# Seven-product gated FFN on one core: T1 in four sums, fifth products side by side, ScalarE copies and buffers moved, a later T4 sum, one copy for the last tile

## The chip, the cores and the metric

The kernel runs on one core of one Trainium2 chip. Its time is device time in microseconds (us), the median of the runs shown. Engines are named as the profile names them: PE (matmul, with its weight loads as PEld), DVE (VectorE), ACT (ScalarE), POOL (GpSimd), SP (the DMA queue of SyncE; ACT has a queue too).

## The reference, cut to what matters

```
x: 1024 tokens x 1024 (D)   w_gate, w_up: 1024 x 3584 (F)   w_down: 3584 x 1024      all bf16
out = (gelu_tanh(x @ w_gate) * (x @ w_up)) @ w_down
```

## The kernel before, in words

Both matrix stages use the seven-product form of a 2x2 block product (Strassen's, in Winograd's variant) in place of eight products; the block sums that it needs are made by DVE, POOL and ACT.

**Stage 1** makes gate and up together. For each of the 28 blocks of 128 columns of F (index i), the block matrix A has the gate weights for the two halves of D (a11, a12) and the up weights for the same halves (a21, a22). B is x transposed: B11 and B21 are the two halves of D for tokens 0 to 511 (tile xt0), B12 and B22 the same for tokens 512 to 1023 (tile xt1). xt0 and xt1 come by two DMA transposes on SP. Each product is four matmuls (KH = 4 slices of 128 rows of D) into one PSUM bank of 128x512. Sums of B are made once: T1 = B12 - B11, T2 = B22 - T1, T3 = B22 - B12, T4 = B21 - T2 (`t_sum`, line 153, on DVE), and an fp32 copy of B22 (line 264, on ACT). Sums of A are made for each block: S1, S3 (`early_sums`, lines 165 and 166), S2 (line 170), S4 (line 174), and C22, a copy of a22 (`copy_a22`, line 177, on ACT). Per block:

- `first_product` (a11 x B11) goes to PSUM bank A, and ACT copies it to E1 (line 186). `second_product` (a12 x B21) is added in the same bank, so it can start only when that copy has read it; then ACT's gelu gives the gate of the first tokens (line 192).
- `seed` (line 198): ACT writes E1 into another bank, X. On X are added in turn the sixth product (S2 x T2; ACT copies the bank to E2, line 213), the seventh (S3 x T3; copied to e3, line 226) and the fourth (C22 x T4; DVE multiplies it with the gate, line 217).
- The fifth product (S1 x T1) opens bank Y. DVE adds e3 to it, which is u1 (line 228); the third product (S4 x B22) is added in Y; DVE adds E2 to it, which is h1 (line 233); ACT takes its gelu (line 235) and DVE multiplies it with u1 (`finish`, line 238).

The order of every engine is written out by hand: each engine runs its instructions in program order, and semaphores join them. Eight blocks (LEAD) have their first and second products before anything else, in pairs: first n, first n+1, second n, second n+1. `ahead` then gives one first and one second product at a time. After LEAD, blocks 0 and 1 go together (fifth, ahead, sixth, seventh, ahead, fourth, third), and from block 2 on a loop does one block at a time. PSUM has eight banks: four (tag p) for warm-up and X, four (tag q) for A and Y in turn. e3 has one buffer, u1 three, h1 two.

**Stage 2** is out = hidden x w_down, with 14 pairs of F blocks as two halves of 7 (JF), four token tiles of 128 (TT) and two column halves of w_down. A product is 56 matmuls (line 359). DVE makes, in this order around the change: new sums for the second chain (lines 414, 415), S4 (line 432), T4 in seven pieces (`t4_sum`, line 389), then T3 and S3 in rings of four buffers (`t3_sum` line 386, `s3_sum` line 382), then the output sums (`store_sum`, line 373). The last product but one (S3 x T3, on X) holds back its last two steps of j (TAIL = 2) to the end; the last product (56 matmuls, t by t) is then added on X, copied to bf16 and sent. Its last tile is copied in halves, one by ACT and one by DVE, and sent in two DMAs of 64 KB.

Of the kernel before, what the change touches and what calls it, by code (L numbers as in the profile page):

```python
# [7 lines left out]
ACT = mybir.ActivationFunctionType  # L8
# [4 lines left out]
def kernel(  # L13
# [18 lines left out]
    nc = tc.nc  # L32
    P = nc.NUM_PARTITIONS
    fp32 = mybir.dt.float32
    f32r = mybir.dt.float32r
    bf16 = mybir.dt.bfloat16

    xf = x.flatten_outer_dims()
    of = out.flatten_outer_dims()
    N, D = xf.shape  # L40
    F = w_gate.shape[1]
    NB = 512
    DT = D // P
    KH = DT // 2
    FT = F // P
    NT = N // P
    DB = 512
    NDB = D // DB
    assert N == 2 * NB and DT % 2 == 0 and D % DB == 0 and FT % 4 == 0
    NWARM = 18  # L50
# [3 lines left out]
    TT = NT // 2  # L54
    JF = KF // 2
# [16 lines left out]
    epool = stage1.enter_context(tc.tile_pool(name="e", bufs=2))  # L72
# [3 lines left out]
    B11, B21 = xt0[:, :KH, :], xt0[:, KH:, :]  # L76
    xt1 = uw.tile([P, DT, NB], bf16, name="xt1", tag="uw")
    B12, B22 = xt1[:, :KH, :], xt1[:, KH:, :]
    WG, WU = {}, {}

    def load_gate(c, queue, lo=0, hi=DT):
        if c not in WG:
            WG[c] = gw.tile([P, DT, 2 * P], bf16, name="gw", tag="gw")
        queue.dma_start(  # L84
            out=WG[c][:, lo:hi, :], in_=wg_r[:, lo:hi, 2 * c * P : (2 * c + 2) * P]
        )
# [15 lines left out]
    def a12(i):  # L102
        return block(WG, 2, i, 1)
# [4 lines left out]
    def a22(i):  # L108
        return block(WU, 4, i, 1)

    def product(ps, lhs, rhs, first=True):
        for k in range(KH):
            nc.tensor.matmul(  # L113
                ps,
                lhsT=lhs[:, k, :],
                rhs=rhs[:, k, :],
                start=(first and k == 0),
                stop=(k == KH - 1),
                skip_group_check=True,
            )  # L120

    def psum_p(name):
        return psum.tile([P, NB], fp32, name=name, tag="p")

    def psum_q(name):
        return psum.tile([P, NB], fp32, name=name, tag="q")

    with tc.manual_schedule():
        zt = opool.tile([P, NB], bf16, name="zt", tag="o")
        nc.vector.memset(zt, 0.0)  # L130
        warm = [psum_p("warm") for _ in range(4)]
        for n in range(NWARM):
            nc.tensor.matmul(warm[n % 4], lhsT=zt[:, 0:P], rhs=zt, start=True, stop=True)

        table = opool.tile([P, 8], bf16, name="table", tag="o")
        nc.scalar.activation(table, zt[:, 0:8], ACT.Gelu_apprx_tanh)

        nc.sync.dma_start_transpose(out=xt0, in_=xf[0:NB, :])  # L138
        load_gate(0, nc.scalar, 0, KH)
        load_gate(0, nc.sync, KH, DT)  # L140
        load_gate(1, nc.sync)
        load_up(0, 0, 2)
# [6 lines left out]
        T = {}  # L149
        for name in ("T1", "T2", "T3", "T4", "B22"):  # L150
            T[name] = xpool.tile([P, KH, NB], f32r, name=name, tag=name)

        def t_sum(name, a, b):
            for k in range(0, KH, 2):
                ks = slice(k, k + 2)
                nc.vector.tensor_tensor(T[name][:, ks, :], a[:, ks, :], b[:, ks, :], ALU.subtract)  # L156

        S1, S2, S3, S4, C22 = {}, {}, {}, {}, {}
# [13 lines left out]
        def late_sums(i, engine=nc.gpsimd):  # L172
            S4[i], C22[i] = weight_tile("s4"), weight_tile("c22")
            engine.tensor_tensor(S4[i], a12(i), S2[i], ALU.subtract)  # L174

        def copy_a22(i):
            nc.scalar.activation(C22[i], a22(i), ACT.Copy)
# [3 lines left out]
        def first_product(i):  # L181
            A[i] = psum_q("a")
            product(A[i], a11(i), B11)
            if i % 2 == 0:
                E1[i // 2] = ring.tile([P, 2, NB], fp32, name="e1", tag="ring")
            nc.scalar.activation(E1[i // 2][:, i % 2, :], A[i], ACT.Copy)  # L186

        def second_product(i):
            product(A[i], a12(i), B21, first=False)
            if i % 2 == 0:  # L190
                GL[i // 2] = half.tile([P, 2, NB], bf16, name="gl0", tag="half")
            nc.scalar.activation(GL[i // 2][:, i % 2, :], A[i], ACT.Gelu_apprx_tanh)  # L192

        X, Y, E2, U1, G1 = {}, {}, {}, {}, {}

        def seed(i):
            X[i] = psum_p("x")
            nc.scalar.activation(X[i], E1[i // 2][:, i % 2, :], ACT.Copy)
# [3 lines left out]
        def ahead():  # L202
            nonlocal done
            if done < FT:
                first_product(done)
            if done:
                second_product(done - 1)
            done += 1
# [10 lines left out]
        def fifth_product(i):  # L219
            Y[i] = psum_q("y")  # L220
            product(Y[i], S1[i], T["T1"])

        def seventh_product(i):
            product(X[i], S3[i], T["T3"], first=False)
            e3 = epool.tile([P, NB], fp32, name="e3", tag="e3", bufs=1)
            nc.scalar.activation(e3, X[i], ACT.Copy)  # L226
            U1[i] = epool.tile([P, NB], bf16, name="u1", tag="u1", bufs=3)
            nc.vector.tensor_tensor(U1[i], Y[i], e3, ALU.add)  # L228

        def third_product(i):  # L230
            product(Y[i], S4[i], T["B22"], first=False)
            h1 = epool.tile([P, NB], bf16, name="h1", tag="h1")
            nc.vector.tensor_tensor(h1, Y[i], E2.pop(i), ALU.add)  # L233
            G1[i] = epool.tile([P, NB], bf16, name="gl1", tag="gl1")
            nc.scalar.activation(G1[i], h1, ACT.Gelu_apprx_tanh)  # L235
# [4 lines left out]
        for i in range(2):  # L240
            early_sums(i, nc.vector)
            second_sum(i)
            late_sums(i, nc.vector)
        t_sum("T1", B12, B11)
        t_sum("T2", B22, T["T1"])
        t_sum("T3", B22, B12)
        t_sum("T4", B21, T["T2"])
# [5 lines left out]
        for n in range(0, LEAD, 2):  # L253
            first_product(n)
            first_product(n + 1)
            second_product(n)
            if n + 2 < LEAD:
                second_product(n + 1)
        done = LEAD
        for i in range(2):  # L260
            copy_a22(i)
            seed(i)
        for k in range(KH):
            nc.scalar.activation(T["B22"][:, k, :], B22[:, k, :], ACT.Copy)
        fifth_product(0)
        fifth_product(1)
        ahead()
        sixth_product(0)
        sixth_product(1)
# [75 lines left out]
        def two(j, base=0):  # L345
            return slice(base + 2 * j, base + 2 * j + 2)
# [5 lines left out]
        B11 = lambda j: V11[j // 2][:, two(j % 2), :]  # L352
        B12 = lambda j: V12[:, two(j), :]
# [14 lines left out]
        def send(t, db, o_sb):  # L368
            nc.sync.dma_start(out=of[t * P : (t + 1) * P, db * DB : (db + 1) * DB], in_=o_sb)
# [6 lines left out]
        X = [psum.tile([P, DB], fp32, name="x", tag="p") for t in range(TT)]  # L376
# [3 lines left out]
        def s3_sum(j):  # L380
            S3[j] = s3pool.tile([P, 2, NB], f32r, name="s3", tag="s3")
            nc.vector.tensor_tensor(S3[j], A11(j), A21(j), ALU.subtract)  # L382

        def t3_sum(j):
            T3[j] = ring.tile([P, 2, DB], f32r, name="t3", tag="ring")
            nc.vector.tensor_tensor(T3[j], B22(j), B12(j), ALU.subtract)  # L386

        def t4_sum(j):
            nc.vector.tensor_tensor(TC[j], B21(j), TC[j], ALU.subtract)  # L389

        def b22_copy(j):
            C22[j] = ring.tile([P, 2, DB], f32r, name="c22", tag="ring")
            nc.scalar.activation(C22[j], B22(j), ACT.Copy)
# [16 lines left out]
        HEAD = 3  # L410
        Y = [psum.tile([P, DB], fp32, name="y", tag="q") for t in range(TT)]
# [28 lines left out]
        for j in range(JF):  # L440
            for t in range(TT):
                step(Y[t], SC[j], C22[j], j, t, last=True)
            if j + RING < JF:
                b22_copy(j + RING)
            else:
                t3_sum(j + RING - JF)
            if HEAD + j < JF:
                t4_sum(HEAD + j)
            nc.scalar.activation(SC[j], A22(j), ACT.Copy)

        TAIL = 2
        for j in range(JF):
            if j < JF - TAIL:
                for t in range(TT):
                    step(X[t], S3[j], T3[j], j, t)
            if j + RING < JF:
                s3_sum(j + RING)
                t3_sum(j + RING)
        for t in range(TT):
            store_sum(t, 1, Y[t], EB[t])  # L460
        for t in range(TT):
# [4 lines left out]
        for t in range(TT):  # L466
            for j in range(JF):
                step(X[t], SC[j], TC[j], j, t, last=True)
            o_sb = opool.tile([P, DB], bf16, name="o_sb", tag="o")
            if t < TT - 1:  # L470
                nc.scalar.activation(o_sb, X[t], ACT.Copy)
                send(TT + t, 0, o_sb)
            else:
                HB = DB // 2
                rows = of[(TT + t) * P : (TT + t + 1) * P, :]
                nc.scalar.activation(o_sb[:, :HB], X[t][:, :HB], ACT.Copy)
                nc.vector.tensor_copy(o_sb[:, HB:], X[t][:, HB:])
                nc.scalar.dma_start(out=rows[:, 0:HB], in_=o_sb[:, :HB])
                nc.sync.dma_start(out=rows[:, HB:DB], in_=o_sb[:, HB:])


# [28 lines left out]
```

## Time and profile before

| | us |
|---|---|
| median of 3 runs | 280.31 (279.88 to 280.32) |
| the profiled execution's own time | 280.14 |
| its span, first to last instruction | 278.4 |
| outside the span | 1.7 |
| PE busy | 271.3 (97%) |
| DVE / ACT / POOL busy | 190.0 / 138.0 / 88.6 |

The granted TensorE clock was 0.999 over the span. A line of the timeline gives start, duration, engine, line, operation, tiles written<-read and how many instructions were merged (x2); in brackets the idle time of the engine just before, and what ended it. A merged row runs from its first start to its last end, and starts of successive instructions lie closer together than one instruction's duration, since they overlap.

### The profile page before, as it was taken

How to read it: one execution, taken by the hardware profiler on the slowest of the kernel's cores; microseconds unless marked ns; L12 is line 12 of the kernel's file. 1: busy time of each engine (PE TensorE's matmuls, PEld its weight loads, DVE VectorE, ACT ScalarE, POOL GpSimd, SP SyncE). 2: the span in 40 equal slices, each digit the busy share in tenths (PEclk: the TensorE clock that was granted, in tenths of full speed). 3: DMA queues.
4: the chain of work that ended last, by engine and by line, in shares of the span. 5: the costliest groups of instructions: out<-in, count | busy, mean ns of one | idle time of the engine just before them, and what ended most of it. 6: DMA issues, size and time to landing. Idle time of an engine off the chain costs nothing.

```text
span 278.4 us, 3314 instructions
## 1 busy us (share of the span) xinstructions
PE 271.3 (97%) x1194; PEld 190.2 (68%) x1194; DVE 190.0 (68%) x226; ACT 138.0 (50%) x236; POOL 88.6 (32%) x81
## 2 busy tenths in 40 slices
PE   8898999999999999999999999999999999999994
PEld 3345677778777786777866677764447888888783
DVE  0179864857567576675766655669994999999800
ACT  2469475565665666556665666632100072860311
POOL 0000284646556475554855444500000000000000
PEclk9999999999999999999999999999999999999999
DMA  7997402242072051242520211359702000000321
GB/s 172 279 261 194 151 4 72 83 146 77 0 226 78 0 173 60 72 133 93 153 75 1 75 41 37 95 173 330 235 0 75 2 0 0 0 2 0 115 75 38
DMA packets 41055, 26.41 MB, mean 95 GB/s; under 512 B 9168, under 2 KB 41040, under 8 KB 41040
## 3 DMA queue, kind: packets, MB, share of 16 engines
q1 hardware_dynamic: 40368, 25.89, 31.8%
q10 hardware_dynamic: 672, 0.33, 0.4%
q8 instruction: 9, 0.15, 0.2%
q14 instruction: 6, 0.05, 0.1%
HBM read 22.02 MB, written 2.10 MB: 87 GB/s over the span
## 4 chain that ended last, share of the span: by engine, by line
PE 74%; DVE 15%; SPq 4%; DMA 3%; issue 2%; ACT 0%; DVEq 0%; ACTq 0%
PE x L113 26%; PE y L113 18%; PE a L113 12%; PE x L359 10%; PE z L359 4%; PE y L359 4%; DMA xt<-in_x_dram 3%; DVE T L156 3%; DVE t L386 3%; DVE tc L389 3%; DVE sc L432 2%; SPq L138 2%; SPq L84 2%; DVE sc L414 1%; DVE s L382 1%
## 5 line engine op out<-in xcount | busy, mean ns | idle before, releaser
L113 PE MATMUL x<-T,s 128*128 128x512 f32 x224 | 63.5, 408 | 0.0
L113 PE MATMUL a<-xt,gw 128*128 128x512 bf16 x224 | 52.2, 380 | 1.2 <-DMA xt<-in_x_dram 1.2
L174 POOL TENSOR_TENSOR s<-gw,s 128x512 fp32r<-128x512 bf16 x26 | 30.4, 1169 | 63.4 <-PE y L113 62.7
L113 PEld LDWEIGHTS x<-T,s 128*128 128x128 f32 x224 | 42.0, 188 | 10.5 <-ACT e L213 0.4
L228 DVE TENSOR_TENSOR u<-y,e 128x512 bf16<-128x512 f32 x28 | 19.4, 691 | 35.3 <-ACT e L226 35.3
L170 DVE TENSOR_TENSOR s<-s,gw 128x512 fp32r<-128x512 f32 x28 | 40.8, 1457 | 0.0
L113 PEld LDWEIGHTS <-gw 128*128 128x128 bf16 x224 | 20.2, 98 | 28.4 <-issue 7.0
L217 DVE TENSOR_TENSOR gT<-gl,x 128x512 bf16<-128x512 bf16 x28 | 19.2, 687 | 18.6 <-PE x L113 18.6
L113 PE MATMUL y<-T,s 128*128 128x512 f32 x112 | 30.2, 391 | 0.8 <-DVE T L156 0.8
L113 PE MATMUL x<-T,c 128*128 128x512 f32 x112 | 30.4, 393 | 0.1
L113 PE MATMUL y<-B,s 128*128 128x512 f32 x112 | 30.0, 391 | 0.0
L235 ACT ACTIVATE gl<-h 128x512 bf16<-128x512 bf16 x28 | 17.7, 631 | 24.3 <-DVE h L233 24.3
L166 POOL TENSOR_TENSOR s<-gw,uw 128x512 fp32r<-128x512 bf16 x25 | 29.3, 1170 | 0.0
L165 POOL TENSOR_TENSOR s<-uw 128x512 fp32r<-128x512 bf16 x25 | 29.1, 1165 | 0.0
L186 ACT ACTIVATE e<-a 128x512 f32<-128x512 f32 x28 | 16.7, 596 | 24.8 <-PE a L113 24.7
L359 PE MATMUL x<-tc,sc 128*128 128x512 f32 x112 | 25.7, 389 | 0.0
L226 ACT ACTIVATE e<-x 128x512 f32<-128x512 f32 x28 | 16.8, 599 | 17.5 <-PE x L113 15.1
L113 PEld LDWEIGHTS y<-T,s 128*128 128x128 f32 x112 | 20.9, 188 | 5.9 <-DVE T L156 1.7
L113 PEld LDWEIGHTS x<-T,c 128*128 128x128 f32 x112 | 20.8, 188 | 5.2 <-ACT e L226 1.0
L113 PEld LDWEIGHTS y<-B,s 128*128 128x128 f32 x112 | 21.0, 188 | 4.8
L359 PEld LDWEIGHTS x<-tc,sc 128*128 128x128 f32 x112 | 21.0, 188 | 4.4
L192 ACT ACTIVATE gl<-a 128x512 bf16<-128x512 f32 x28 | 16.7, 597 | 7.3 <-PE a L113 7.2
(51 smaller groups left out, 315.8 us busy)
## 6 DMA issues: line engine op xcount, KB each, us to landing
gw<-in_w_gate_dram SPq DMA_DIRECT2D x13, 512.0 KB, 4.0
uw<-in_w_up_dram SPq DMA_DIRECT2D x6, 1024.0 KB, 6.4
v<-in_w_down_dram SPq DMA_DIRECT2D x5, 512.0 KB, 3.7
v<-in_w_down_dram SPq DMA_DIRECT2D x4, 640.0 KB, 8.8
v<-in_w_down_dram SPq DMA_DIRECT2D x8, 256.0 KB, 3.9
out_dram<-o_sb SPq DMA_DIRECT2D x15, 128.0 KB, 1.7
uw<-in_w_up_dram SPq DMA_DIRECT2D x2, 512.0 KB, 5.9
gw<-in_w_gate_dram ACTq DMA_DIRECT2D x1, 256.0 KB, 4.2
```

The costliest lines, as they stand in the source:

```text
L113: nc.tensor.matmul(ps, lhsT=lhs[:, k, :], rhs=rhs[:, k, :], start=(first and k == 0), stop=(k == KH - 1), skip_group_check=True,)
L165: engine.tensor_tensor(S1[i], a21(i), a22(i), ALU.add)
L166: engine.tensor_tensor(S3[i], a11(i), a21(i), ALU.subtract)
L170: nc.vector.tensor_tensor(S2[i], S1[i], a11(i), ALU.subtract)
L174: engine.tensor_tensor(S4[i], a12(i), S2[i], ALU.subtract)
L186: nc.scalar.activation(E1[i // 2][:, i % 2, :], A[i], ACT.Copy)
L192: nc.scalar.activation(GL[i // 2][:, i % 2, :], A[i], ACT.Gelu_apprx_tanh)
L217: nc.vector.tensor_tensor(gT[:, i, 0:NB], GL[i // 2][:, i % 2, :], X[i], ALU.mult)
L226: nc.scalar.activation(e3, X[i], ACT.Copy)
L228: nc.vector.tensor_tensor(U1[i], Y[i], e3, ALU.add)
L235: nc.scalar.activation(G1[i], h1, ACT.Gelu_apprx_tanh)
L359: nc.tensor.matmul(ps, lhsT=lhs[:, i, t * P : (t + 1) * P], rhs=rhs[:, i, :], start=(first and j == 0 and i == 0), stop=(last and j == JF ...
```

## The change

It has these parts:

1. `table` activation, xt0's transpose and the first gate load stand ahead of the warm-up matmuls in the text.
2. T1 is made in four sums of 128x512 in place of two of 128x1024 (T2, T3 and T4 stay at two).
3. The fifth products of blocks 0 and 1 are interleaved by slice k: block 0 and block 1 with T1's slice 0, then both with slice 1, and so on.
4. `copy_a22` and `seed` of blocks 0 and 1 go into the LEAD loop: block 0's after the second products of blocks 2 and 3, block 1's after those of 4 and 5. They stood behind the loop, ahead of the B22 copies.
5. e3 gets two buffers in place of one, u1 two in place of three, h1 one in place of two.
6. In stage 2 the last piece of T4 is made behind the last S3 and T3 sums.
7. The last output tile is copied by ACT in one piece and sent in one DMA of 128 KB from ACT's queue.

```
-        t_sum("T1", B12, B11)
+        t_sum("T1", B12, B11, 1)
...
             if n + 2 < LEAD:
                 second_product(n + 1)
+            if n in (2, 4):
+                copy_a22(n // 2 - 1)
+                seed(n // 2 - 1)
         done = LEAD
-        for i in range(2):
-            copy_a22(i)
-            seed(i)
         for k in range(KH):
             nc.scalar.activation(T["B22"][:, k, :], B22[:, k, :], ACT.Copy)
-        fifth_product(0)
-        fifth_product(1)
+        for i in range(2):
+            Y[i] = psum_q("y")
+        for k in range(KH):
+            for i in range(2):
+                nc.tensor.matmul(
+                    Y[i],
+                    lhsT=S1[i][:, k, :],
+                    rhs=T["T1"][:, k, :],
+                    start=(k == 0),
+                    stop=(k == KH - 1),
...
-            e3 = epool.tile([P, NB], fp32, name="e3", tag="e3", bufs=1)
+            e3 = epool.tile([P, NB], fp32, name="e3", tag="e3")
...
-            U1[i] = epool.tile([P, NB], bf16, name="u1", tag="u1", bufs=3)
+            U1[i] = epool.tile([P, NB], bf16, name="u1", tag="u1")
...
-            h1 = epool.tile([P, NB], bf16, name="h1", tag="h1")
+            h1 = epool.tile([P, NB], bf16, name="h1", tag="h1", bufs=1)
...
-            if HEAD + j < JF:
+            if HEAD + j < JF - 1:
                 t4_sum(HEAD + j)
...
                 t3_sum(j + RING)
+        t4_sum(JF - 1)
         for t in range(TT):
             store_sum(t, 1, Y[t], EB[t])
...
-            if t < TT - 1:
-                nc.scalar.activation(o_sb, X[t], ACT.Copy)
-                send(TT + t, 0, o_sb)
-            else:
-                HB = DB // 2
-                rows = of[(TT + t) * P : (TT + t + 1) * P, :]
-                nc.scalar.activation(o_sb[:, :HB], X[t][:, :HB], ACT.Copy)
-                nc.vector.tensor_copy(o_sb[:, HB:], X[t][:, HB:])
-                nc.scalar.dma_start(out=rows[:, 0:HB], in_=o_sb[:, :HB])
-                nc.sync.dma_start(out=rows[:, HB:DB], in_=o_sb[:, HB:])
+            nc.scalar.activation(o_sb, X[t], ACT.Copy)
+            queue = nc.sync if t < TT - 1 else nc.scalar
+            queue.dma_start(out=of[(TT + t) * P : (TT + t + 1) * P, 0:DB], in_=o_sb)
```

More of the change, by code (lines that the diff above doesn't have):

```diff
@@ L131 @@
         warm = [psum_p("warm") for _ in range(4)]
-        for n in range(NWARM):
-            nc.tensor.matmul(warm[n % 4], lhsT=zt[:, 0:P], rhs=zt, start=True, stop=True)
         table = opool.tile([P, 8], bf16, name="table", tag="o")
@@ L139 @@
         load_gate(0, nc.scalar, 0, KH)
+        for n in range(NWARM):
+            nc.tensor.matmul(warm[n % 4], lhsT=zt[:, 0:P], rhs=zt, start=True, stop=True)
         load_gate(0, nc.sync, KH, DT)
@@ L151, with t_sum @@
             T[name] = xpool.tile([P, KH, NB], f32r, name=name, tag=name)
-        def t_sum(name, a, b):
-            for k in range(0, KH, 2):
-                ks = slice(k, k + 2)
+        def t_sum(name, a, b, step=2):
+            for k in range(0, KH, step):
+                ks = slice(k, k + step)
                 nc.vector.tensor_tensor(T[name][:, ks, :], a[:, ks, :], b[:, ks, :], ALU.subtract)
@@ L258 @@
                 second_product(n + 1)
+            if n in (2, 4):
+                copy_a22(n // 2 - 1)
+                seed(n // 2 - 1)
         done = LEAD
-        for i in range(2):
-            copy_a22(i)
-            seed(i)
         for k in range(KH):
             nc.scalar.activation(T["B22"][:, k, :], B22[:, k, :], ACT.Copy)
-        fifth_product(0)
-        fifth_product(1)
+        for i in range(2):
[8 more added lines that the diff above has]
+                    stop=(k == KH - 1),
+                    skip_group_check=True,
+                )
         ahead()
```

## The prediction

> **What bounds the kernel.** The page's first part and the waits of PE, in this order:
>
> ```profile
> PE 271.3 (97%) x1194; PEld 190.2 (68%) x1194; DVE 190.0 (68%) x226; ACT 138.0 (50%) x236; POOL 88.6 (32%) x81
> ```
>
> ```profile
> PE a L113 <- DMA xt<-in_x_dram: 1.2, 1, 1.2
> ...
> PE y L113 <- DVE T L156: 0.8, 2, 0.4
> PE x L359 <- DVE t L386: 0.3, 1, 0.3
> ```
>
> PE is busy nearly throughout, and waits in three places. Two belong to the change: the fifth products for T1, and stage 2 for a T3 sum. So a microsecond counts only if it closes a hole of PE, and the holes are read from the timeline. PE's pace comes from whole rows without a hole: eight fp32 matmuls take 1.99 us ("33.71 1.99 PE y x8"), 2.19 when they follow bf16 ones ("38.90 2.19 PE x x8"), 56 take 12.86 ("236.05 12.86 PE y x56"); so one starts each 0.227, a bf16 one each 0.216 (ACT's copies behind four come 0.86 apart).
>
> **T1 and the fifth products.** The timeline from 20.8 us:
>
> ```profile
> 20.35 2.36 DVE L156 TENSOR_TENSOR T<-xt,xt 128x1024 fp32r<-128x1024 bf16 x2 [1.99 <-DMA xt<-in_x_dram]
> ...
> 20.44 0.81 PE L113 MATMUL a<-xt,gw 128*128 128x512 bf16 x3
> ...
> 21.63 0.73 PE L113 MATMUL y<-T,s 128*128 128x512 f32 x2 [0.38 <-DVE T L156]
> ...
> 22.77 1.65 PE L113 MATMUL y<-T,s 128*128 128x512 f32 x6 [0.40 <-DVE T L156]
> ```
>
> LEAD's last matmuls start at 20.44 + 3 x 0.216, so PE is free at 21.09. It waits for T1's first half (to 21.58), then for its second (to 22.72), and ends at 24.42. Without holes the eight would end at 21.09 + 1.99 = 23.08: 1.34 us are lost, 0.78 as waits and the rest in the pipe's restarts (a matmul behind a wait takes 0.34 to the next, not 0.227).
>
> In quarters: DVE's 128x512 sums (lines 165, 166) last 0.69 and start 0.60 apart, so T1's slices are ready at 21.05, 21.65, 22.25 and 22.85, plus 0.05 for the semaphore. A half of 128x1024 costs 1.14 start to start, two quarters 1.20, so T2 to T4 and the sums behind them come 0.13 later. They have room: T4 ended at 29.52, the fourth product needs it at 31.28.
>
> [...]
>
> **Copies in LEAD.** The other half of this sum. ACT in LEAD:
>
> ```profile
> 14.38 0.60 ACT L192 ACTIVATE gl<-a 128x512 bf16<-128x512 f32 x1 [0.27 <-PE a L113]
> 15.25 0.60 ACT L192 ACTIVATE gl<-a 128x512 bf16<-128x512 f32 x1 [0.27 <-PE a L113]
> 16.11 0.60 ACT L186 ACTIVATE e<-a 128x512 f32<-128x512 f32 x1 [0.27 <-PE a L113]
> ```
>
> 15.25 is the gelu of block 3, 16.11 the E1 copy of block 4. That copy ends at 16.71, and block 4's second product, which adds into the same bank, starts at 16.78 with the hand-over of 0.05: no slack. ACT's idle time is 0.27 per instruction; now a copy_a22 and a seed come between. After a gelu they start 0.49 and 0.52 apart, and the next instruction 0.52 later (21.29, 21.78, 22.30, 22.82). So E1 starts at 15.25 + 0.49 + 0.52 + 0.52 = 16.78 in place of 16.11, ends at 17.38, and second product 4 starts at 17.43: a new hole of 0.65. What is queued behind the seed is E1 of blocks 4 and 5, and only PE waits for it. The same comes behind block 5's gelu: 1.30 in all. PE leaves LEAD at 22.39, not 21.09.
>
> There T1's slices 0 to 2 lie ready and slice 3 is (22.90) before it is needed (23.75). The eight matmuls run without a hole, and end at 22.39 + 1.99 = 24.38 against 24.42. **The two parts cancel: 0.03 gained.** Bounds: with no hole in LEAD, the fifth products would follow T1: slice 3 at 22.90, its two matmuls to about 23.6, gain 0.8. With holes of the whole time that ACT is taken (1.04 each for two steps of 0.52), 2.08 in all, the end is 25.16, loss 0.74. I take the middle: start-to-start rows give it. ACT later has two copies and two seeds less ahead of B22: nobody waited for those (e2 of block 0 starts 0.04 behind its matmul, at 27.12).
>
> **The second e3 buffer.** Timeline from 28.9:
>
> ```profile
> 28.99 0.60 ACT L226 ACTIVATE e<-x 128x512 f32<-128x512 f32 x1 [0.35 <-PE x L113]
> ...
> 31.24 0.69 DVE L228 TENSOR_TENSOR u<-y,e 128x512 bf16<-128x512 f32 x1
> ...
> 31.28 2.59 PE L113 MATMUL x<-T,c 128*128 128x512 f32 x8
> 32.03 0.60 ACT L226 ACTIVATE e<-x 128x512 f32<-128x512 f32 x1 [2.43 <-DVE u L228]
> ```
>
> e3 of block 1 waits for the only buffer, which u1 of block 0 reads late, since DVE is in T4 and the sums of block 2 until 31.24. Fourth product 1 can't add into X until that copy is done, at 32.63: the row of eight takes 2.59 where 2.19 is due. With two buffers the copy runs at about 29.9, long before its bank is needed at 32.4. **Gain 0.40.** Next late: u1 of blocks 0 and 1 (31.37 to 32.66 with the 0.13), needed by third products at 33.3 and 34.2, so nothing. Elsewhere e3's single buffer held nobody: that wait occurs once.
>
> h1 with one buffer: h1 of block 1 now waits for gelu 0 (0.63), some 0.5 later than now (35.73). Behind it on DVE stand finish 0, S2 of block 3 and, after 1.83 idle, u1 of block 2. PE needs its bank for first product 10 about 0.4 after its end, and E2 of block 2, behind gelu 1 on ACT, ends 0.3 before seventh product 2. Cost 0; without this cover up to 0.2. Later h1 comes once a block (4.5 to 6.3 us), gelu long done. u1 with two: finish of i-2 stands ahead of u1 of i on DVE. Part 1 changes no engine's order, so costs nothing.
>
> From here to 215 us PE runs at its pace, so the gain is carried; DVE in stage 2 starts at 215.39 from a PE release, and moves along.
>
> **T4's last piece.**
>
> ```profile
> 257.41 1.21 DVE L386 TENSOR_TENSOR t<-v,v 128x1024 fp32r<-128x1024 bf16 x1
> 258.55 1.28 DVE L373 TENSOR_TENSOR o_sb<-y,eb 128x512 bf16<-128x512 f32 x2
> 258.68 0.77 PEld L359 LDWEIGHTS x<-t,s 128*128 128x128 f32 x4 [0.68 <-DVE t L386]
> ```
>
> DVE runs without a gap from 215.39 to here, and PE waits for its last T3: the product's 42 + 14 matmuls, begun at 248.74, end at 262.15, 13.41 where 12.86 is due. One sum (1.14) leaves this queue, so T3 is ready at 257.5 (on the way S3 of j = 4 waits 0.16 for PE's first step, inside that), and PE wants it at 258.26. **Gain 0.53.** T4's piece then ends at 258.62, where T3 ended, and the last product wants it at about 264; store sums start as now. Bounds: 0 if S3's ring waits instead, 0.55.
>
> **The last tile.**
>
> ```profile
> 274.88 0.38 ACT L476 ACTIVATE o_sb<-x 128x256 bf16<-128x256 f32 x1 [2.58 <-PE x L359]
> 275.29 0.36 ACTq L478 DMA_DIRECT2D out_dram<-o_sb  x1
> 275.29 0.42 DVE L477 CAST o_sb<-x 128x256 bf16<-128x256 f32 x1 [11.12 <-ACT o_sb L476]
> 275.75 0.33 SPq L479 DMA_DIRECT2D out_dram<-o_sb  x1
> ```
>
> DVE's half came behind ACT's, not beside it; the last DMA was issued at 275.75. One copy takes 0.60 (line 471): issue at 275.51, 0.24 earlier. Landing was 1.6 for 64 KB on SP, 1.7 for 128 KB there and for 64 KB on ACT's queue; 128 KB on ACT's queue isn't shown: between 1.7 and 1.9. Gain 0.1 (0 to 0.15).
>
> **Sum.** 0.03 + 0.40 + 0.53 + 0.10 = 1.06 from the profiled execution's 280.14 gives 279.1 (the median, 280.31, lies 0.17 above it). Less than 0.2%, 0.56 us, can't be told from no change.
>
> **Rivals.**
> - LEAD's copies cost PE nothing (E1 isn't what second products wait for). T1 then pays: 0.8 for 0.03, so 278.3. Against it: the 0.07 between E1's end and the product, repeated over LEAD. 0.12.
> - LEAD's holes outgrow T1's: 1.04 each, 0.74 lost for 0.03 gained: 279.9. 0.12.
> - T4's piece goes but S3 or T3 waits for PE's ring: the 0.53 is missing, 279.6. 0.09.
> - Slower: the new holes close the clock. The warm-up's first matmuls started 0.43 apart for 3.4 us, then 0.216; a fall in LEAD would cost 3.4 us at half pace, 1.7: 280.8. [...] 0.07.
>
> [...]
>
> The forecast has 0.60. Faster is the forecast and the first rival, 0.72; same the second and third, 0.21; slower 0.07. The range goes from the first rival less 0.1 to the second, 278.2 to 279.9, and leaves out the last.
>
> **What would show it.** Right: E1 of block 4 near 16.8 and two PE holes of 0.65 at 16.8 and 20.9 to 21.5; y's eight in 2.0 us with no wait, the next a at 24.2; x<-T,c x8 in 2.2; no PE wait at line 386's T3; the last DMA issued 0.63 after the last copy starts. Wrong: y still waits for T1 (LEAD had no holes), or holes over 0.8, or a new wait on h1 at 36 to 37 us.

## The result and the profile after

The changed kernel takes 279.12 us (median of 6 runs, 278.69 to 279.34) against 280.09 of the kernel before (6 runs, 279.88 to 280.32): ratio 0.9963, 95% interval 0.9950 to 0.9976. The profiled execution took 279.10, span 277.3; that is 1.04 below the profiled execution of before, where 1.06 was worked out.

The waits of PE after the change, the answer to the waits shown before (columns: total us, times, longest):

```profile
PE a L113 <- DMA xt<-in_x_dram: 0.9, 1, 0.9
...
PE a L113 <- ACT e L185: 0.8, 2, 0.5
```

Both waits that the prediction started from, for T1 and for T3, are gone. A new one stands in their place: two times, PE's bf16 products (line 113) wait for ACT's copy to E1 (line 185, 186 before). The timeline of the changed kernel from 14 us shows where:

```profile
15.27 0.60 ACT L191 ACTIVATE gl<-a 128x512 bf16<-128x512 f32 x1 [0.27 <-PE a L113]
...
15.77 0.62 ACT L176 ACTIVATE c<-uw 128x512 fp32r<-128x512 bf16 x1
...
16.29 0.59 ACT L197 ACTIVATE x<-e 128x512 f32<-128x512 f32 x1
...
16.81 1.08 ACT L185 ACTIVATE e<-a 128x512 f32<-128x512 f32 x2
...
17.45 3.61 PE L113 MATMUL a<-xt,gw 128*128 128x512 bf16 x16 [0.32 <-ACT e L185]
...
20.47 2.50 DVE L155 TENSOR_TENSOR T<-xt,xt 128x512 fp32r<-128x512 bf16 x4 [1.92 <-DMA xt<-in_x_dram]
...
21.54 1.02 PE L113 MATMUL a<-xt,gw 128*128 128x512 bf16 x4 [0.48 <-ACT e L185]
...
22.21 2.18 PE L268 MATMUL y<-T,s 128*128 128x512 f32 x8
```

The ACT column reads as one queue: gelu of block 3, copy_a22, seed, and only then E1 of block 4, at 16.81. The product that needs it starts at 17.45. The same again ends at 21.54. The fifth products (line 268) then run as one row of 2.18 without a wait, and end at 24.39, where they ended at 24.42 before.

Further on in the same trace, the fourth products and the e3 copy in front of them:

```profile
29.89 0.60 ACT L225 ACTIVATE e<-x 128x512 f32<-128x512 f32 x1 [0.32 <-PE x L113]
...
31.24 2.19 PE L113 MATMUL x<-T,c 128*128 128x512 f32 x8
...
35.76 0.69 DVE L232 TENSOR_TENSOR h<-y,e 128x512 bf16<-128x512 f32 x1 [0.70 <-ACT gl L234]
```

The row of eight takes 2.19 (2.59 before). The last line is the price of h1's single buffer: DVE waits 0.70 for gelu 0, once, and PE's next rows follow without a wait. PE in stage 2, and the end:

```profile
248.41 12.86 PE L368 MATMUL x<-t,s 128*128 128x512 f32 x56
261.10 12.86 PE L368 MATMUL x<-tc,sc 128*128 128x512 f32 x56
```

```profile
273.99 0.60 ACT L480 ACTIVATE o_sb<-x 128x512 bf16<-128x512 f32 x1 [2.58 <-PE x L368]
274.62 0.36 ACTq L482 DMA_DIRECT2D out_dram<-o_sb  x1
```

The product with S3 and T3 is one row of 56 in 12.86 (two rows, 13.41 in all, before). On DVE its last T3 sum (line 395) now stands ahead of T4's last piece (line 398), and ends at 257.32; it ended at 258.62 before:

```profile
256.10 1.22 DVE L395 TENSOR_TENSOR t<-v,v 128x1024 fp32r<-128x1024 bf16 x1
257.24 1.22 DVE L398 TENSOR_TENSOR tc<-v,tc 128x1024 fp32r<-128x1024 bf16 x1
```

The last DMA is issued 0.63 after the last copy starts (0.87 before).

So the gain stands in three places: block 1's fourth product, the last T3, the last tile. At T1 and the fifth products, which parts 2 to 4 of the change touch, PE is where it was. The experiments ask whether these edits cancel for the reason given.

### The profile page after: what moved, and what is told of

The parts are those of the page before. It is cut to its first block, busy times and chain, and to the rows that moved or that the text cites. A ratio compares the mean times of both kernels' runs of the same rounds, so it can differ in the third digit from the quotient of the medians.

```text
span 277.3 us, 3341 instructions
## 1 busy us (share of the span) xinstructions
PE 271.0 (98%) x1194; PEld 190.2 (69%) x1194; DVE 189.3 (68%) x227; ACT 138.1 (50%) x236; POOL 88.7 (32%) x81
## 4 chain that ended last, share of the span: by engine, by line
PE 94%; DMA 3%; ACT 2%; issue 0%
PE x L113 28%; PE x L368 18%; PE y L113 18%; PE a L113 17%; PE y L368 9%; PE z L368 4%; DMA xt<-in_x_dram 3%; PE y L268 1%; ACT gl L191 0%; ACT e L185 0%; ACT c L176 0%; ACT x L197 0%; ACT o_sb L480 0%
## 5 line engine op out<-in xcount | busy, mean ns | idle before, releaser
L113 PE MATMUL a<-xt,gw 128*128 128x512 bf16 x224 | 52.8, 380 | 1.7 <-DMA xt<-in_x_dram 0.9
L113 PE MATMUL y<-T,s 128*128 128x512 f32 x104 | 27.8, 389 | 0.0
L113 PEld LDWEIGHTS y<-T,s 128*128 128x128 f32 x104 | 19.5, 188 | 4.1
```

The costliest lines, as they stand in the source:

```text
L113: nc.tensor.matmul(ps, lhsT=lhs[:, k, :], rhs=rhs[:, k, :], start=(first and k == 0), stop=(k == KH - 1), skip_group_check=True,)
```

## The experiments

My theory, as in the prediction: second products wait for E1, and E1 queues behind copies on ACT, so the copies in LEAD cost what T1's quarters give; e3's buffer, T4's place and the last tile make the gain. The rivals: the copies are free and the quarters pay; or the interleaving pays; or one of the late edits moves its wait elsewhere.

All ratios are to the kernel before in the same runs. For places in the trace, note that T1's first sum starts when xt1 has landed, between 19.98 and 20.70 us in the 14 profiles of this study, also in kernels with the same loads. So a place early in the trace is told from that start, as in "seventh product at T1 + 7.48", which is where the kernel before has it. Where PE leaves LEAD late, as in the changed kernel, its places don't follow T1, and such a distance carries T1's spread.

| kernel | us (runs) | ratio, 95% interval |
|---|---|---|
| changed (again) | 278.93 (5) | 0.9953, 0.9941 to 0.9966 |
| lead_only | 280.19 (10) | 1.0000, 0.9991 to 1.0009 |
| t1_only | 280.29 (10) | 1.0003, 0.9993 to 1.0013 |
| t1_in_order | 278.88 (4) | 0.9956, 0.9942 to 0.9969 |
| parts_5_6_7 | 278.88 (5) | 0.9955, 0.9942 to 0.9967 |
| e3_only | 279.95 (10) | 0.9990, 0.9981 to 1.0000 |
| t4_only | 279.66 (10) | 0.9984, 0.9974 to 0.9993 |
| tail_only | 280.17 (10) | 0.9999, 0.9989 to 1.0008 |
| no_lead | 278.77 (5) | 0.9955, 0.9943 to 0.9968 |
| late_b22 | 278.22 (5) | 0.9936, 0.9922 to 0.9949 |
| late_again (the same) | 278.29 (5) | 0.9930, 0.9916 to 0.9943 |
| late_halves | 278.85 (5) | 0.9950, 0.9938 to 0.9963 |

**The copies in LEAD alone.** The kernel before with this edit:

```
         if n + 2 < LEAD:
             second_product(n + 1)
+        if n in (2, 4):
+            copy_a22(n // 2 - 1)
+            seed(n // 2 - 1)
     done = LEAD
-    for i in range(2):
-        copy_a22(i)
-        seed(i)
```

> The kernel before with copies and seeds of blocks 0 and 1 in LEAD and nothing else; T1 in two halves. My theory: two holes of 0.65 in LEAD, PE arrives at the fifth products at 22.4, T1's second half (22.77) is ready at 22.85 when it is needed, so both waits for T1 are gone and the fifth products end at 24.4 as before: 0.0 gained, 280.1 us. The fourth product of block 1 starts at 32.7 as before, held by e3's one buffer. Rival (the holes add to the waits, only quarters hide them): 0.7 to 1.3 slower at the fifth products' end.

280.19: no difference. PE in its timeline:

```profile
17.16 3.61 PE L113 MATMUL a<-xt,gw 128*128 128x512 bf16 x16 [0.48 <-ACT e L186]
21.26 1.02 PE L113 MATMUL a<-xt,gw 128*128 128x512 bf16 x4 [0.48 <-ACT e L186]
21.93 2.20 PE L113 MATMUL y<-T,s 128*128 128x512 f32 x8
```

The holes are there, and the fifth products run without a wait with T1 in halves too. So the copies hide T1's wait by making PE late, and with them the quarters have next to nothing to remove. Halves are only just in time: T1 began early in this execution, at 20.07, its second half ended at 22.43, and the third matmul, the first to read it, started at 22.58. With T1 at 20.41 to 20.55, as in the profiles that have LEAD's copies and quarters, halves would come up to 0.2 late (an estimate from these rows).

**T1 in quarters and fifth products side by side, alone**, in the kernel before:

```
-        t_sum("T1", B12, B11)
+        t_sum("T1", B12, B11, 1)
...
-        fifth_product(0)
-        fifth_product(1)
+        (the loop over k, then i, of the change)
```

> The kernel before with T1 in quarters and the fifth products side by side, nothing else. My theory: the fifth products end near 23.5 (24.27 before), but e2 is late on ACT (seventh product near 27.6) and the fourth product of block 1 waits, through e3's one buffer, for DVE's u1 of block 0, which the quarters put 0.13 later: that product starts at 32.8 (32.68 before), so all of T1's 0.8 is lost and the time is 280.2, 0.1 above before. Rival (T1's waits are worth what they show): 0.8 faster, 279.3.

280.29: no gain, as the theory had it. Its timeline:

```profile
26.40 0.59 ACT L192 ACTIVATE gl<-a 128x512 bf16<-128x512 f32 x1
26.88 1.09 ACT L213 ACTIVATE e<-x 128x512 f32<-128x512 f32 x2
...
27.53 1.66 PE L113 MATMUL x<-T,s 128*128 128x512 f32 x6 [0.36 <-ACT e L213]
```

```profile
31.03 1.27 PE L113 MATMUL x<-T,c 128*128 128x512 f32 x4
32.76 1.20 PE L113 MATMUL x<-T,c 128*128 128x512 f32 x4 [0.46 <-ACT e L226]
```

The fifth products do end early (the next product starts at T1 + 3.13; before, at T1 + 3.91). Then the lead is lost in two steps. ACT, still behind with copies, seeds and B22, reaches E2 late, and the seventh product (27.53) waits for it: T1 + 7.24, so 0.24 of the 0.78 is left. And the fourth product of block 1 waits for the one e3 buffer, whose time is set by DVE: T1 + 12.46, against T1 + 12.32 before: 0.14 later, what quarters cost DVE.

**The fifth products in order again**, in the changed kernel:

```
-        for i in range(2):
-            Y[i] = psum_q("y")
-        for k in range(KH):
-            for i in range(2):
-                nc.tensor.matmul(...)
+        fifth_product(0)
+        fifth_product(1)
```

> The changed kernel with the fifth products one block after the other again (T1 still in quarters). My theory: after LEAD's holes PE arrives at 22.4, T1's last quarter (22.9) is there before block 0 needs it (23.07), so the order is worth nothing: y's eight in 2.0 us, 279.1 us. Rival (side by side is what removed the wait for T1): a wait for T1 comes back, 0.3 to 0.5 slower, 279.5.

278.88, and no wait for T1; its row of fifth products takes 2.19:

```profile
21.56 1.02 PE L113 MATMUL a<-xt,gw 128*128 128x512 bf16 x4 [0.48 <-ACT e L185]
22.23 2.19 PE L113 MATMUL y<-T,s 128*128 128x512 f32 x8
```

Side by side is worth nothing that these runs can show here.

**Only parts 5, 6 and 7**, in the kernel before:

```
-            e3 = epool.tile([P, NB], fp32, name="e3", tag="e3", bufs=1)     # and u1 3 to 2, h1 2 to 1
+            e3 = epool.tile([P, NB], fp32, name="e3", tag="e3")
...
-            if HEAD + j < JF:
+            if HEAD + j < JF - 1:
                 t4_sum(HEAD + j)
...
+        t4_sum(JF - 1)
...
-            if t < TT - 1: ... else: (two halves)
+            nc.scalar.activation(o_sb, X[t], ACT.Copy)
+            queue = nc.sync if t < TT - 1 else nc.scalar
+            queue.dma_start(...)
```

> The kernel before with e3's second buffer (u1 two, h1 one), T4's last sum later and the last tile in one copy; T1 in halves, fifth products in order, copies behind LEAD. My theory: T1's quarters, the fifth products' order and the copies in LEAD bring nothing between them, so this is as fast as the changed kernel: 0.40 + 0.55 + 0.2 below before, 279.1 us. Rival (the three early parts carry some of the gain): 0.3 or more slower than the changed kernel.

278.88 (278.70 to 279.25), beside the changed kernel's 278.93 (278.69 to 279.03) on the same chip: the early parts, 1 to 4, bring nothing between them that this spread would show, and a net of 0.7 either way, as in the prediction's bounds, is excluded. Its trace still has the old waits for T1 (0.8 in two), and no holes in LEAD.

**Each of these three hunks alone**, in the kernel before.

> The kernel before with e3 two buffers, u1 two, h1 one. My theory: the row of eight fourth-product matmuls takes 2.19 in place of 2.59, 0.40 gained, 279.7 us; h1's one buffer puts h1 of block 1 about 0.5 later and costs PE nothing there. In the changed kernel 0.12 of the lead was lost again between 39 and 150 us in steps of some 0.02; if the buffers do that, this kernel loses it too, if not it keeps 0.40. Rival (DVE holds the fourth products otherwise): under 0.1.

> The kernel before with T4's last sum behind the last S3 and T3, nothing else. My theory: PE's wait for T3 at 258.7 goes, 56 matmuls in 12.86 in place of 13.41: 0.55 gained, 279.5 us. Rival (the wait moves to another sum of the ring or to the last product): under 0.2 gained.

> The kernel before with the last tile in one copy and one DMA, nothing else. My theory: the last DMA is issued 0.63 after the copy starts in place of 0.87, landing 1.7 as for 64 KB on ACT's queue: 0.2 gained (the changed kernel showed 0.24 at issue and 0.20 at the span's end). Rival (a larger DMA on one queue lands later): 0 to 0.1 slower.

e3_only: 279.95, 0.31 below before (280.26), with an interval that just reaches 1; h1's and u1's buffers were changed with e3's, and not alone. t4_only: 279.66, 0.60 below. Their rows, the fourth products of the first and the S3 x T3 product of the second:

```profile
31.51 2.19 PE L113 MATMUL x<-T,c 128*128 128x512 f32 x8
```

```profile
248.50 12.86 PE L359 MATMUL x<-t,s 128*128 128x512 f32 x56
```

0.40 and 0.55 on PE, as expected. tail_only: 280.17, 0.09 below, which its interval does not tell from zero; its profile shows the last DMA issued 0.63 after the copy starts and 1.7 to landing for 128 KB. From the last copy's start to the span's end the trace has 3.31 us in place of 3.48 (3.33 in the changed kernel). So at the end of the trace 0.15 to 0.17 is gained, but the times can't confirm it. The 0.20 in the expectation comes from this end too, and is a little too much.

The 0.12 that e3_only was also to settle: between the sixth product of block 2 and stage 2's first matmul, the kernel before took 150.91 us and the changed one 151.02. Over all 14 profiles this stretch takes 150.91 to 151.03, and both ends occur with old buffers and with new ones (t1_only and tail_only, with the old ones, 151.03; the changed kernel again, 150.91). It is the spread of executions, not a cost of the buffers.

**Can the cancelled gain be had?** First, the copies back behind LEAD in the changed kernel:

```
-            if n in (2, 4):
-                copy_a22(n // 2 - 1)
-                seed(n // 2 - 1)
         done = LEAD
+        for i in range(2):
+            copy_a22(i)
+            seed(i)
```

> The changed kernel with copy_a22 and seed of blocks 0 and 1 put back behind LEAD. My theory (second products wait for E1, E1 queues behind copies on ACT): both new holes of 0.65 us in LEAD vanish, PE is free at about 21.1, the fifth products follow T1's quarters and end near 23.5 in place of 24.2 - but ACT then reaches e2 of block 0 only near 26.9, behind two copies, two seeds and four B22 copies, so the seventh product starts near 27.55 in place of 27.81: 0.2 to 0.3 better than the changed kernel, 278.9 us. Rival (LEAD's copies cost PE nothing): time as the changed kernel, 279.1, and the holes are still there. Second rival (nothing on ACT is late): 0.75 better, 278.4.

278.77, which is not told from the changed kernel. The holes in LEAD are gone, the fifth products end at T1 + 3.13, and the seventh product starts at T1 + 7.28 (the changed kernel 7.34):

```profile
26.85 0.59 ACT L191 ACTIVATE gl<-a 128x512 bf16<-128x512 f32 x1
27.32 1.09 ACT L212 ACTIVATE e<-x 128x512 f32<-128x512 f32 x2
...
27.98 1.21 PE L113 MATMUL x<-T,s 128*128 128x512 f32 x4 [0.40 <-ACT e L212]
```

ACT is the next bound: gelu and E2 stand in its queue without idle time, behind four B22 copies, and PE waits. I had expected 0.2 to 0.3 from this; the wait of 0.40 and the slower restart behind it left 0.02 to 0.06 at this product (the changed kernel's repeat has it at T1 + 7.30).

Then the B22 copies, which only the third products need (at 33 us), are moved out of the way:

```
         done = LEAD
         for i in range(2):
-            copy_a22(i)
             seed(i)
-        for k in range(KH):
-            nc.scalar.activation(T["B22"][:, k, :], B22[:, k, :], ACT.Copy)
+        for i in range(2):
+            copy_a22(i)
+        b22_part(0, 1)        # one of the four copies
...
         seventh_product(1)
+        b22_part(1, KH)       # the other three
         ahead()
```

> The changed kernel with the copies and seeds of blocks 0 and 1 behind LEAD (seeds first), one B22 copy behind them, and the other three B22 copies behind the seventh products. My theory: LEAD has no hole, ACT is on time for e2 of block 0 (due 26.3), so the fifth products end near 23.5, the seventh product starts near 27.05 (27.81 in the changed kernel), where DVE's T3 is just ready: 0.75 better than the changed kernel, 278.35 us. Rival (DVE's chain T1 to T4 bounds this stage, not ACT): the seventh products wait for T3 or the fourth for T4, and no more than 0.3 is gained, 278.8 or above.

278.22, and 278.29 in the repeat, for which was expected:

> The kernel with the copies behind LEAD and three B22 copies behind the seventh products, once more beside the changed kernel: 0.8 to 0.95 below it, 278.2 us.

In the repeat it stands 0.64 below the changed kernel (278.93), where 0.8 to 0.95 was expected. This kernel beats both. The repeat's timeline:

```profile
20.55 2.50 DVE L155 TENSOR_TENSOR T<-xt,xt 128x512 fp32r<-128x512 bf16 x4 [1.96 <-DMA xt<-in_x_dram]
...
21.30 2.54 PE L272 MATMUL y<-T,s 128*128 128x512 f32 x8
...
25.23 4.10 PE L113 MATMUL x<-T,s 128*128 128x512 f32 x16
...
27.64 0.31 PEld L113 LDWEIGHTS x<-T,s 128*128 128x128 f32 x2 [0.15 <-DVE T L155]
```

The sixth and seventh products are one row of 4.10 again, and begin at T1 + 4.68 (25.78 - 20.47 = 5.31 in the changed kernel, 5.27 in its repeat): 0.59 to 0.63 earlier, the size of the difference in time. That it fits so closely is partly luck, since PE's place in the changed kernel doesn't follow T1. The seventh's weight load waits 0.15 for T3 (a matter of the loads alone, PE's row has no hole); DVE's chain of T sums may be the next bound, which no run here tests.

Last, the same kernel with T1 in halves and the fifth products in order:

```
-        t_sum("T1", B12, B11, 1)
+        t_sum("T1", B12, B11)
...
-        (the loop over k, then i)
+        fifth_product(0)
+        fifth_product(1)
```

> The same kernel with T1 in halves and the fifth products in order. My theory: quarters and order pay where LEAD has no hole: PE waits again 0.8 for T1's halves, the seventh product comes 7.45 us after T1's first sum starts in place of 6.71, and the time is 0.75 above that kernel, 279.0 us. Rival (ACT's order alone made the gain): within 0.2 of that kernel.

278.85, 0.56 slower than late_again beside it, where 0.75 was expected; both waits for T1 (0.8) are back, and the seventh product starts at T1 + 7.52 in place of 6.72. So quarters and order pay once neither LEAD's holes nor ACT's queue stand behind them. ACT's order alone, without them, gives nothing over parts_5_6_7 (278.88).

The changed kernel itself was run again with these:

> The changed kernel once more, so that the next ones stand beside it on one chip: 279.1 us, 1.0 below the kernel before.

278.93, 1.24 below before (280.17), a little more than in the first runs (0.97); the intervals of the ratios overlap.

## Why the prediction was right, step by step

- **LEAD's copies.** Right, in size too. E1 of block 4 at 16.81 (16.78 was worked out), the product behind it at 17.45 (17.43), and PE out of LEAD at 21.54 + 4 x 0.216 = 22.40 (22.39). Two waits for gate loads, 0.14 and 0.15, which before didn't have, lay in LEAD of this execution as well; the second took its time out of the first hole, since ACT's queue, not PE, sets when that ends. That PE's place came out to 0.01 is luck: PE began LEAD 0.15 earlier than before (7.99 against 8.14), which the first of these waits took back.
- **T1 and the fifth products.** Right in what it says, that the two parts cancel: the end moved from 24.42 to 24.39, and both bounds (0.8 gained, 0.74 lost) are excluded. That it moved by just the 0.03 of the forecast is luck: the product behind the fifth products starts at 23.98 to 24.27 in the four profiles with LEAD's copies, and at 23.89 to 24.48 in the six with T1 in halves and no copies there. The row reads 2.18 and not 2.0, since it starts inside the last bf16 matmul, as the prediction's own row of 2.19 does; from 22.40 to 24.39 it is 1.99. One reading in the prediction is off: of the 1.34 lost before, restarts take two times 0.11 and not 0.56; the rest lies in the waits, which the profile counts from a matmul's end (0.39 behind its start) and not from where the next was due (0.227).
- **Quarters and order.** What the prediction didn't say: interleaving and quarters were then all but idle. With LEAD's holes, halves are in time where T1 starts early (lead_only) and order doesn't matter (t1_in_order). The 0.13 that quarters cost DVE was 0.14 in t1_only. One quarter lasts 0.69 and one half 1.22; since they overlap, the four took 2.50 together in the changed kernel and the two 2.36 before.
- **"Nobody waited for those", of ACT's copies ahead of B22.** True in the kernel before and in the changed one. It fails once PE comes 0.8 earlier: t1_only and no_lead wait there (0.36 and 0.40). So the first rival, 278.3 if LEAD's copies were free, had the wrong condition: taking them out gave 278.77. It took the move of the B22 copies besides, and then 278.22 to 278.29 came.
- **e3's second buffer.** 0.40 on PE, as worked out; 0.31 in time, alone.
- **h1's one buffer.** h1 of block 1 waited for gelu 0 as said (0.70), and PE had no wait there.
- **"From here to 215 us PE runs at its pace, so the gain is carried".** 0.45 at 35 us had become 0.33 in stage 2. That is the spread of executions over this stretch (150.91 to 151.03), with no line of the kernel behind it.
- **T4's last piece.** 0.55 on PE for 0.53; no wait came in its place.
- **The last tile.** Right, or a little small: 0.10 forecast, 0.15 at the span's end. 128 KB on ACT's queue landed in 1.74 (64 KB on SP, before, in 1.60), near the lower of the two values allowed. In time it can't be told from nothing.
- **The clock.** The slower rival did not come: behind the first hole 16 bf16 matmuls take 3.61, so they start 0.216 apart as they did ahead of it, and behind the second the fifth products take 2.18. The 3.4 us at half pace in that rival was an estimate from the warm-up, and no row here shows such a stretch behind a hole: behind the hole at the warm-up's end in the kernel before (1.60 from start to start, 6.54 to 8.14) bf16 matmuls start 0.215 to 0.216 apart. The clock row of the profile's page can't decide this: it has 9 in every slice, the warm-up's too, where matmuls started 0.43 apart.

The sum was met to 0.02 by the profiled executions (1.04 for 1.06). By their traces it is 0.03 at the fifth products, 0.42 at the fourth, 0.55 at T3 and 0.15 at the end, less 0.11 over the long stretch; the few hundredths that three of these had too little in the forecast made up for most of the 0.11, which is luck. The medians fell by 0.97, and by 1.24 in the repeat.

## What to carry to other kernels

Before a wait is priced as a gain, ask what the engine behind it will meet next: here T1's 1.34 us was worth nothing alone, because E2 on ACT and then e3's buffer behind DVE stood 4 and 9 us later, each late by most of the same time, and 0.6 once both were cleared. Before an instruction is put into an engine's idle time, ask what slack the next one in its queue has: here 0.27 us of idle between ACT's copies, with 0.07 between a copy's end and the product that needs it, was no room for 1.04. And two edits that cancel can move a wait in the profile with the time unchanged: here the holes of PE's ahead of the fifth products took the place of their wait, 0.8 for E1 in place of 0.8 for T1.

## What the runs showed of the hardware that was not expected

- The prediction read from one trace that a matmul behind a wait takes 0.34 to the next one, not 0.227. In that trace it is so for fp32 matmuls, at 21.63, 22.77, 32.68 and 258.68; the bf16 ones behind the changed kernel's two holes start 0.215 apart. In late_again the restart comes back at each quarter of T1, 0.33 to 0.34 four times, though none of these waits is long enough to stand among PE's. The row's 2.54 is set by T1's pace, though: pairs of matmuls start at 21.30, 21.90, 22.50 and 23.10, the 0.60 apart at which DVE makes the quarters, and only the last restart adds to it.
- The landing of xt1, and so T1's start, moved by 0.7 us (19.98 to 20.70) between executions with the same loads in the same order. With copies in LEAD, PE reaches the fifth products late in any case (21.93 in lead_only, 22.21 in the changed kernel, 22.23 in t1_in_order); kernels that wait for T1 move with it (fifth products 0.75 behind its start in late_b22 and in late_again, where T1 starts at 20.15 and 20.55). It is a spread of the size of most effects here, and one reason to read places in the trace from T1's start.
